# Forgetting attention with a spectral mix: two loads of v on hardware queues, and two late copies exchanged between ScalarE and VectorE

## The chip, the cores and the metric

The kernel runs on one core of one Trainium2 chip. The metric is the device time of one execution in microseconds. A core has five engines that run beside each other, each with its own instruction queue: TensorE (PE; its weight loads are shown as PEld), VectorE (DVE), ScalarE (ACT), GpSimd (POOL) and SyncE (SP), which here only issues transfers. All transfers run on 16 DMA engines. Transfers are issued from GpSimd ([...]the profile calls that queue q0), from SP (q1) or from ScalarE (q10). Matrix products land in PSUM, and VectorE or ScalarE copy them from there to SBUF.

## The reference

```python
scores = scale * np.matmul(q, k.transpose(0, 1, 3, 2))        # B=8, H=8, S=576, head_dim 64
cum = np.cumsum(np.log(np.clip(f, 0.0001, 1.0)), axis=-1)
scores = np.where(causal, -1e9, scores + cum[:, :, :, None] - cum[:, :, None, :])
attn = softmax(scores)
x = np.matmul(attn, v)            # then as (B, S, H * D): 8 x 576 x 512
X = np.fft.rfft(x, axis=1)        # the first 64 modes are kept
Yr = Xr @ w_r - Xi @ w_i          # for each mode m: one 512 x 512 matrix w_r[m] and w_i[m]
Yi = Xr @ w_i + Xi @ w_r
y = np.fft.irfft(Y, n=S, axis=1)
u = x + y
return u + np.maximum(u @ w_ch, 0.0)
```

All inputs and the output are float32. q, k, v are 9.4 MB each, the two mode weights 67 MB each, the output 9.4 MB.

## The kernel before

**Attention.** The 64 pairs of batch and head are worked in 32 steps; two steps (the two heads of a pair of heads) share one load of k, q and v, so there are 16 such loads, called pairs here: pair 0 is loaded first, then pair 1, and so on. `emit_loads(pr)` (L260) issues the three transfers of pair `pr` into a staging buffer; three staging buffers rotate, and the one of pair 1 lies in the tile wx, which later holds weights. k and q are cast to bf16 on the way, which only GpSimd's queue does here; v is kept in float32 and is not cast. Of v, only pair 0 goes another way: line 270 sends it to SP's queue (L271). Everything else goes through `pool_dma` (L91), which also pins the transfer into the written order of GpSimd's queue. The first use of a pair is a copy that rearranges k, q or v (L482, L486), followed by transposes (L500) and their copies out of PSUM (L513, L515, L517), scores (L552), the exponential on ScalarE (L559), a triangular mask on VectorE (L574) and the product with v (L597), which VectorE divides by its sum into `x_all` (L608, L619).

**The head.** Before the first pair is used, the decay is computed from f: f is loaded by SP (L292), ScalarE takes the logarithm (L344), VectorE the running sum (L349), and after transposes and subtractions ScalarE takes two exponentials (L389, L412). The result scales v at L486.

**Modes.** The weights w_r and w_i come as 128 transfers of 512 KB of bf16 (cast from 1 MB of float32; the last two of them in halves) through GpSimd's queue, in an order fixed in `tile_of` and `emit_w_load`, into nine rotating buffers. `emit_modes` (L170, L186) multiplies one such pair of tiles with the transformed x. The first tiles are loaded beside the attention. A weight's buffer comes free when its products are done, and GpSimd waits for that, and for the landing of an earlier transfer, before it issues the next.

**The inverse transform and the last product.** z = x @ w_ch is computed in parallel to the last weights (`emit_xw`, `XW`, L838, L845). The modes' results y, and y @ w_ch, come in parts: the early part is added to `x_all` and `XW` in `emit_part` (L887, L888) while weights still arrive. What remains for the end is the late part of y, in three groups. The last group depends on the last weights. Its rows are made at L1017 by `y_rows`: four transposes into the PSUM tile ply (y itself, bf16) and four products into plw (y @ w_ch, called the z rows here, float32). Each holds 128 partitions: 16 rows for each of the eight batch entries. They must go to the tile `yy`, to partitions that differ with the batch entry. For batch 0 a copy does that directly (`row_slot(0, t, ...)`, t = 0 for y, 1 for z); for the other seven the whole 128 rows are copied to a stage `yls[0]` and moved from there by 14 transfers of 16 KB, issued by GpSimd (`emit_moves`, L801): first the two for batch 1, then the rest. Then 20 jobs produce the output: TensorE adds x and the late part of y into the PSUM tiles pu and pz (L806), ScalarE copies pu (L974), VectorE computes max(pz, 0) + u (L981), and SP and ScalarE store it (L988, L993).

**What sets the order.** Each engine runs its instructions in one fixed order. Except where `tc.keep_in_program_order` pins an instruction behind the one written before it on its engine (GpSimd's transfers, the rearranging copies of the first three pairs, the last modes' products), a planner of the compiler may move an instruction ahead of others that are ready later by its own estimate. It also adds the waits: an instruction that reads a PSUM tile waits for what wrote it, and two engines that touch one PSUM tile are kept apart.

The lines that the change replaces:

```python
                if nm == "v" and pr < 1:
                    nc.sync.dma_start(dst, ap)
...
        nc.vector.tensor_copy(row_slot(0, 0, H2, H4), ply[0:H4, :])
        nc.scalar.copy(yls[0][:, 0, :], ply[:, :])
        emit_moves(yls[0], H2, 1, 0, nc.gpsimd)
        run(terms(jobs[0], ps, 0, "y"))
        nc.vector.tensor_copy(row_slot(0, 1, H2, H4), plw[0:H4, :])
        nc.vector.tensor_copy(yls[0][:, 1, :], plw[:, :])
        emit_moves(yls[0], H2, 1, 1, nc.gpsimd)
```

Of the kernel before, what the change touches and what calls it, by code (L numbers as in the profile page):

```python
# [21 lines left out]
def kernel(  # L22
# [11 lines left out]
    nc = tc.nc  # L34
# [55 lines left out]
    def pool_dma(dst, src):  # L90
        tc.keep_in_program_order(nc.gpsimd.dma_start(dst, src))  # L91
# [133 lines left out]
    with ExitStack() as actx:  # L225
# [34 lines left out]
        def emit_loads(pr):  # L260
            dc, bp, _ = steps[2 * pr]
            for nm, src in (("k", k), ("q", q), ("v", v)):
                one = src[2 * bp, 2 * dc, :, :]
                dst = QKVst[pr % STG][nm][:, :, :, :].rearrange("p b r d -> p b (r d)")
                ap = bass.AP(
                    tensor=one.tensor,
                    offset=one.offset,
                    ap=[[NR * Dh, 128], [H * S * Dh, 2], [1, NR * Dh]],
                )
                if nm == "v" and pr < 1:  # L270
                    nc.sync.dma_start(dst, ap)  # L271
                else:
                    pool_dma(dst, ap)

# [2 lines left out]
        def scratch(parts, *dims):  # L277
# [13 lines left out]
        ft = ftf[:BH, :]  # L291
        nc.sync.dma_start(ft[:], f.rearrange("b h s -> (b h) s"))  # L292
        emit_loads(0)
        nc.gpsimd.memset(trimask[:, :], 1.0)
        nc.gpsimd.affine_select(
# [15 lines left out]
            channel_multiplier=-1,  # L311
        )
        emit_loads(1)
        emit_w_load(0)
        emit_w_load(1)
# [378 lines left out]
        for s in range(NS + 1):  # L694
            pr, h = s // 2, s % 2
            if s == 0:
                emit_loads(STG - 1)
# [35 lines left out]
    with ExitStack() as bctx:  # L733
        bsb = bctx.enter_context(tc.tile_pool(name="bsb", bufs=1))
        YTe = bsb.tile([128, NDC, B, HM], BF16, name="YTe")
        H2, H4 = HM // 2, HM // 4
# [42 lines left out]
        def row_slot(b, t, r0, n):  # L779
            p0 = HM * ((b + t) % 2) + r0  # L780
            return yy[p0 : p0 + n, 1, b // 2, t, :]
# [17 lines left out]
        def emit_moves(yl, r0, b, t, eng):  # L799
            p0 = H4 * b  # L800
            ins = eng.dma_start(row_slot(b, t, r0, H4), yl[p0 : p0 + H4, t, :])  # L801
            if eng is nc.gpsimd:
                tc.keep_in_program_order(ins)
# [147 lines left out]
        def terms(job, ps, t, what):  # L951
            b, _, nb = job
            rows = [[] for _ in range(2 * nb)]
            for tt, i, o, hs, src, basis in pieces(job):
                if tt != t:
                    continue
                p = ps[t][o, i, :]
                rows[2 * i].append((p, ident_bf[hs, hs], src, True))
                rows[2 * i + 1].append((p, basis, yy[hs, 1, b // 2, t, :], False))
            return [r for k, r in enumerate(rows) if "xy"[k % 2] in what]  # L960

        def run(*lists, pin=False):
            for k in range(max(len(l) for l in lists)):
                for l in lists:
                    for a in l[k] if k < len(l) else ():
                        ins = add(*a)
                        if pin:
                            tc.keep_in_program_order(ins)
# [45 lines left out]
        ply = psL.tile([128, D], F32, tag="A", name="ply")  # L1014
        ply = ply[:, 0 : D // 2].bitcast(BF16)
        plw = psL.tile([128, D], F32, tag="A", name="plw")
        y_rows(YTl, 0, ply[:, :], plw[:, :])  # L1017
        nc.vector.tensor_copy(row_slot(0, 0, H2, H4), ply[0:H4, :])
        nc.scalar.copy(yls[0][:, 0, :], ply[:, :])
        emit_moves(yls[0], H2, 1, 0, nc.gpsimd)  # L1020
        run(terms(jobs[0], ps, 0, "y"))
        nc.vector.tensor_copy(row_slot(0, 1, H2, H4), plw[0:H4, :])
        nc.vector.tensor_copy(yls[0][:, 1, :], plw[:, :])
        emit_moves(yls[0], H2, 1, 1, nc.gpsimd)
        for b in range(2, B):
# [60 lines left out]
```

The softmax here doesn't subtract the row's maximum and nothing guards it: scores larger than these inputs give would overflow.

## Time and profile before

| | |
|---|---|
| six runs | median 438.12 us (436.19 to 439.43) |
| the profiled execution | 438.14 us, span 436.4 us |
| mean granted TensorE clock | 0.834 |
| PE busy | 368.2 us (84% of the span) |
| DVE busy | 263.5 us (60%) |
| ACT busy | 225.3 us (52%) |
| POOL busy | 129.1 us (30%) |
| transfers | 97.37 MB at the destination; 163.73 MB read from HBM, 9.44 MB written to it |

The profile is of one execution, and its times count from the start of the span. The slices of the page cut the span into 40 equal parts of 10.9 us; a digit is the busy share in tenths. A line of the timeline gives the start, the duration, the engine (SPq, ACTq and POOLq are the engine's queue, where a transfer's issue counts), the line of the program, the operation with its output and inputs, the number of instructions merged, and in brackets the idle time of the engine just before and what ended it. A line of the table by stretches gives the stretch, its length, the busy time and count of instructions of PE, PEld, DVE, ACT and POOL, the granted clock of TensorE, the share in which the 16 DMA engines were busy, and GB/s at the destination; the share can pass 1, because packets of one engine overlap. A wait for several events is put down to the one that came last.

### The profile page before, as it was taken

To read this page: it belongs to the slowest core of one execution; us is meant where nothing else is said; L and a number is where in the kernel's file an instruction comes from. 1 tells how busy PE (TensorE), PEld (TensorE's weight loads), DVE (VectorE), ACT (ScalarE), POOL (GpSimd) and SP (SyncE) were. 2 spreads that over 40 slices of the span, in tenths; PEclk is the share of its full clock that TensorE was granted. 3 is DMA by queue.
4 is the path that set the end of the run, shared out by engine and by line. 5 is a ranking of instruction groups with operands and counts; after the bars stand their busy time and mean duration, and the time that the engine had idled before them with its cause. 6 is when DMAs were issued, how large, how long until landed. Compare 5 with 4: busy or idle time off the path is not lost.

```text
span 436.4 us, 12232 instructions
## 1 busy us (share of the span) xinstructions
PE 368.2 (84%) x5265; PEld 250.9 (57%) x5265; DVE 263.5 (60%) x658; ACT 225.3 (52%) x340; POOL 129.1 (30%) x202
## 2 busy tenths in 40 slices
PE   2687699999897978878878798799999988798993
PEld 1454566776666656666656676666655544454451
DVE  5687788877555654556656577624323655553874
ACT  3688377875635446364364654143444444542762
POOL 7333332153233232332332222232232232200500
PEclk9997699998856755587566879599999999998997
DMA  8999999999999999999999999999999999993697
GB/s 188 232 236 244 231 237 238 236 214 234 236 211 237 229 219 237 211 236 235 212 237 211 212 211 211 213 210 210 211 213 210 211 211 211 211 210 77 237 390 262
DMA packets 50693, 97.37 MB, mean 223 GB/s; under 512 B 3760, under 2 KB 12944, under 8 KB 50640
## 3 DMA queue, kind: packets, MB, share of 16 engines
q0 software_dynamic: 46688, 86.16, 100.7%
q1 hardware_dynamic: 3632, 9.91, 6.1%
q8 instruction: 41, 0.67, 0.6%
q10 hardware_dynamic: 320, 0.52, 0.5%
q14 instruction: 12, 0.10, 0.1%
HBM read 163.73 MB, written 9.44 MB: 397 GB/s over the span
## 4 chain that ended last, share of the span: by engine, by line
PE 31%; DMA 30%; ACT 12%; DVE 9%; issue 4%; POOL 2%; DVEq 0%; POOLq 0%; ACTq 0%
DMA wb<-in_moe_w_i_dram 25%; ACT E L559 8%; PE pav L597 7%; PE ps L552 6%; PE A L186 5%; PE tp L500 5%; DMA stv<-in_v_dram 3%; PE px L640 2%; PE vp L524 2%; ACT KT L513 2%; DVE QTs L515 2%; ACT VT L517 1%; DVE XT L654 1%; DMA yy<-yl 1%; POOL yy L801 1%
## 5 line engine op out<-in xcount | busy, mean ns | idle before, releaser
L559 ACT ACTIVATE E<-ps 128x1024 bf16<-128x1024 f32 (+1 forms) x128 | 101.5, 854 | 25.9 <-PE ps L552 16.6
L91 POOL DMA_DIRECT2D wb<-in_moe_w_r_dram x64 | 42.5, 665 | 132.7 <-PE A L186 28.6
L186 PE MATMUL A<-XT,wb 128*128 128x16 bf16 x1984 | 70.0, 181 | 11.2 <-DMA wb<-in_moe_w_i_dram 6.6
L186 PEld LDWEIGHTS <-wb 128*128 128x128 bf16 x1984 | 63.4, 99 | 25.4 <-issue 11.4
L552 PE MATMUL ps<-QTs,KT 64*128 64x64 bf16 (+4 forms) x384 | 58.0, 326 | 14.4 <-ACT E L559 13.1
L91 POOL DMA_DIRECT2D wb<-in_moe_w_i_dram x64 | 42.5, 664 | 73.4 <-DMA wb<-in_moe_w_i_dram 32.2
L597 PE MATMUL pav<-va,E 128*128 128x65 bf16 (+1 forms) x1088 | 56.2, 212 | 4.4 <-DVE x_all L619 3.6
L597 PEld LDWEIGHTS <-E 128*128 128x128 bf16 (+1 forms) x1088 | 46.5, 117 | 17.6 <-issue 7.1
L574 DVE TENSOR_TENSOR E<-E,trimask 128x256 bf16<-128x256 bf16 (+2 forms) x128 | 37.2, 302 | 19.5 <-ACT E L559 19.3
L517 ACT COPY VT<-tp 128x640 bf16<-128x640 bf16 (+1 forms) x32 | 23.1, 758 | 32.5 <-PE tp L500 32.4
L845 ACT CAST XW<-pxw 128x512 bf16<-128x512 f32 x36 | 20.7, 587 | 35.9 <-PE pxw L838 35.8
L552 PEld LDWEIGHTS <-KT 64*128 64x128 bf16 x384 | 19.5, 100 | 31.0 <-issue 22.4
L888 ACT CAST XW<-pB 128x512 bf16<-128x512 f32 x36 | 21.0, 586 | 29.6 <-PE pB L806 22.4
L838 PE MATMUL pxw<-wch,yy 128*128 128x512 bf16 x144 | 36.0, 388 | 0.0
L887 DVE CAST x_all<-pA 128x512 bf16<-128x512 f32 x36 | 24.9, 692 | 15.4 <-PE pA L806 14.5
L513 ACT COPY KT<-tp 128x640 bf16<-128x640 bf16 (+1 forms) x32 | 22.2, 757 | 22.1 <-PE tp L500 22.1
L515 DVE COPY QTs<-tp 128x640 bf16<-128x640 bf16 (+1 forms) x32 | 23.2, 766 | 14.2 <-PE tp L500 14.1
L619 DVE TENSOR_TENSOR x_all<-pav,rcp 128x384 bf16<-128x384 f32 x64 | 29.1, 455 | 0.8
L608 DVE RECIPROCAL rcp<-pav 128x6 f32<-128x6 f32 x64 | 12.1, 190 | 24.1 <-PE pav L597 23.3
L151 DVE TENSOR_TENSOR YTe<-A,Yacc 128x128 bf16<-128x128 f32 x16 | 5.9, 367 | 33.4 <-PE A L186 33.4
L981 DVE SCALAR_TENSOR_TENSOR uo<-pz,uo 128x1024 f32<-128x1024 f32 (+1 forms) x21 | 21.9, 1069 | 5.0 <-PE pu L806 1.6
L806 PEld LDWEIGHTS <-ident_bf 64*64 64x64 bf16 (+1 forms) x300 | 15.3, 108 | 15.5 <-issue 7.6
(141 smaller groups left out, 641.4 us busy)
## 6 DMA issues: line engine op xcount, KB each, us to landing
wb<-in_moe_w_r_dram POOLq DMA_DIRECT2D x62, 512.0 KB, 16.6
wb<-in_moe_w_i_dram POOLq DMA_DIRECT2D x62, 512.0 KB, 17.5
out_dram<-uo SPq DMA_DIRECT2D x15, 512.0 KB, 4.2
stv<-in_v_dram POOLq DMA_DIRECT2D x10, 576.0 KB, 15.2
stk<-in_k_dram POOLq DMA_DIRECT2D x11, 288.0 KB, 15.1
stq<-in_q_dram POOLq DMA_DIRECT2D x11, 288.0 KB, 15.1
wx<-in_v_dram POOLq DMA_DIRECT2D x5, 576.0 KB, 15.1
wx<-in_k_dram POOLq DMA_DIRECT2D x5, 288.0 KB, 14.7
```

The source lines that it names most:

```text
L91: tc.keep_in_program_order(nc.gpsimd.dma_start(dst, src))
L186: nc.tensor.matmul(A[:, eb, mi, :], lhsT=w_of(mi, eb * 128), rhs=x_of(m), start=(i == 0), stop=(i == len(terms) - 1),)
L513: nc.scalar.copy(rows(KTs[pr % 2][:, :, 0:S]), tv)
L515: nc.vector.tensor_copy(rows(QT[pr][:, :, :]), tv)
L517: nc.scalar.copy(rows(VTs[pr % 2][:, :, 0:S]), tv)
L552: nc.tensor.matmul(ps[:, b, o : o + n], lhsT=KTs[pr % 2][bs, h, jb * 128 : (jb + 1) * 128], rhs=QT[pr][bs, h, jb * 128 + c0 : jb * 128 + c ...
L559: nc.scalar.activation(E[:, :, piece * 512 : piece * 512 + w], ps[:, :, 0:w], ACT.Exp, scale=scale,)
L574: nc.vector.tensor_tensor(dg, dg, tr, ALU.mult)
L597: nc.tensor.matmul(pav[64 * half : 64 * half + w, slot, :], lhsT=E[:, b, c : c + (w - 1) * st + 1 : st], rhs=va[:, jb, b, :], start=(n == ...
L619: nc.vector.tensor_tensor(xo, pi, ri, ALU.mult)
L838: nc.tensor.matmul(pxw[:, :], lhsT=xT[:, eb, i * 128 : (i + 1) * 128], rhs=wch[:, eb, :], start=(eb == 0), stop=(eb == NDC - 1),)
L887: nc.vector.tensor_copy(xs, pA[:, :])
```

## The change

v of pair 0 goes from SP's queue to ScalarE's (the Activation queue). v of pair 1 goes from GpSimd's queue to SP's, where it follows f; it leaves GpSimd's pinned order. At the end, the copy of the whole y rows from ply to the stage goes from ScalarE to VectorE, and the copy of batch 0's z rows from plw goes from VectorE to ScalarE. Sizes and types of all transfers and copies stay as they were.

```diff
-                if nm == "v" and pr < 1:
-                    nc.sync.dma_start(dst, ap)
+                if nm == "v" and pr < 2:
+                    (nc.sync if pr else nc.scalar).dma_start(dst, ap)
                 else:
                     pool_dma(dst, ap)
...
         nc.vector.tensor_copy(row_slot(0, 0, H2, H4), ply[0:H4, :])
-        nc.scalar.copy(yls[0][:, 0, :], ply[:, :])
+        nc.vector.tensor_copy(yls[0][:, 0, :], ply[:, :])
         emit_moves(yls[0], H2, 1, 0, nc.gpsimd)
         run(terms(jobs[0], ps, 0, "y"))
-        nc.vector.tensor_copy(row_slot(0, 1, H2, H4), plw[0:H4, :])
+        nc.scalar.copy(row_slot(0, 1, H2, H4), plw[0:H4, :])
         nc.vector.tensor_copy(yls[0][:, 1, :], plw[:, :])
         emit_moves(yls[0], H2, 1, 1, nc.gpsimd)
```

## The prediction

> **What bounds the kernel now.** I read the page's DMA slices first, because all weights come in once and nothing else in the page runs near its limit for long.
>
> ```profile
> DMA  8999999999999999999999999999999999993697
> GB/s 188 232 236 244 231 237 238 236 214 234 236 211 237 229 219 237 211 236 235 212 237 211 212 211 211 213 210 210 211 213 210 211 211 211 211 210 77 237 390 262
> ...
> q0 software_dynamic: 46688, 86.16, 100.7%
> ```
>
> From the second slice to the 36th the 16 DMA engines never fall below nine tenths. The queue that GpSimd fills (q0) is alone 100.7% of their span. A table of busy time by stretches says the same more finely:
>
> ```profile
> 0.00:2.00 2.00, 0.00 (x0) 0.00 (x0) 1.05 (x8) 1.20 (x1) 0.87 (x5) 1.00 0.00 0
> ...
> 240.00:280.00 40.00, 32.45 (x556) 25.80 (x554) 27.66 (x74) 19.00 (x32) 10.07 (x15) 0.76 1.12 211
> ...
> 394.00:398.00 4.00, 3.78 (x70) 2.39 (x70) 1.89 (x4) 1.17 (x2) 0.00 (x0) 1.00 0.65 128
> ```
>
> The last two columns are the DMA share and GB/s. With weights alone the rate is a flat 211 GB/s of bf16 written, so a 512 KB load takes 524 KB / 211 = 2.48 us; yet the page gives such loads 16.6 and 17.5 us from issue to landing, so some six others stand ahead of each. The whole input as a sum: 163.73 MB read, less 9.44 MB of v and 0.15 MB of f, is 154.1 MB of fp32 that is cast on the way, 77 MB written at 211 GB/s, 365 us; v at the 385 GB/s shown below 24.5 us; f 0.4 us. Together 390 us, in the 397 us between the first traffic (2.2 us) and the last weight (399.45 us). Most of the rest is the end, where the engines finish unevenly (share 0.65). So **one unbroken stream of loads sets the time up to 399.5 us**, and 37 us of output follow. The chain of waits names PE, ScalarE and VectorE for half the span, but it can follow GpSimd's waits for free buffers, which cost nothing while six loads are queued. Only two places can then matter: how soon the stream fills, and what follows its end.
>
> The start, as the GB/s line of the first 20 us in bins of 0.5 us, and as a timeline:
>
> ```profile
> GB/s 0 0 0 0 92 272 230 290 334 313 200 198 201 203 210 201 205 210 198 219 235 373 424 358 255 210 209 217 209 213 201 213 221 213 201 213 213 221 205 201
> ```
>
> ```profile
> 0.80 0.60 SPq L292 DMA_DIRECT2D Yacc<-in_f_dram  x1
> ...
> 1.33 0.87 POOL L91 DMA_DIRECT2D stk<-in_k_dram  x1 [0.82 <-POOLq L1070]
> ...
> 1.47 0.56 SPq L271 DMA_DIRECT2D stv<-in_v_dram  x1
> ...
> 3.75 0.68 ACT L344 ACTIVATE Yacc<-Yacc 64x576 f32<-64x576 f32 x1 [1.67 <-DMA Yacc<-in_f_dram]
> ...
> 5.30 0.73 POOL L91 DMA_DIRECT2D wx<-in_v_dram  x1
> ```
>
> Until 5.0 us only SP's two transfers flow (f, v of pair 0), at 230 to 334 GB/s; from 5 us GpSimd's cast loads run at their usual 200 to 210. The step 373, 424, 358 near 11 us is v of pair 1 passing through GpSimd's queue: uncast, 385 GB/s in the mean, 590 KB in 1.5 us.
>
> The end:
>
> ```profile
> 400.97 0.41 DVE L1018 COPY yy<-ply 16x512 bf16<-16x512 bf16 x1 [0.85 <-PE ply L787]
> ...
> 401.42 0.59 ACT L1019 COPY yl<-ply 128x512 bf16<-128x512 bf16 x1 [3.97 <-DVE yy L1018]
> ...
> 402.60 0.51 POOL L801 DMA_DIRECT2D yy<-yl  x1 [17.80 <-ACT yl L1019]
> 402.68 0.68 DVE L1022 CAST yy<-plw 16x512 bf16<-16x512 f32 x1 [1.29 <-PE plw L791]
> ...
> 403.39 0.69 DVE L1023 CAST yl<-plw 128x512 bf16<-128x512 f32 x1
> 403.43 0.56 PE L806 MATMUL pu<-x_all,ident_bf 64*64 64x512 bf16 x1
> ...
> 403.68 2.02 ACT L974 COPY uo<-pu 128x512 f32<-128x512 f32 x3 [1.67 <-PE pu L806]
> ...
> 404.38 6.22 POOL L801 DMA_DIRECT2D yy<-yl  x13 [1.26 <-DVE yl L1023]
> ...
> 404.80 3.72 DVE L981 SCALAR_TENSOR_TENSOR uo<-pz,uo 128x512 f32<-128x512 f32 x4 [0.71 <-ACT uo L974]
> ```
>
> TensorE runs almost without a gap from 400.33 us to about 408 us, at a granted clock of 0.57 in 400 to 404 us. The first uo on VectorE waits for the products, and from there VectorE is busy 21.9 of 26.1 us.
>
> [...]where SP's last packets and GpSimd's first ones meet, after 5 us, the rate is no higher than later with GpSimd's queue alone. [...]SP's issue at 0.80 is followed by traffic in the bin from 2.0 us, and GpSimd's k, issued at 1.33, by the cast rate only from 5.0. [...]L1019 only reads ply, as L1018 does, and starts 0.04 us after L1018 ends. Its new counterpart on plw will be serial too.
>
> **The change, part by part.** *v of pair 0 to the Activation queue.* One issue, 0.56 us, leaves SP and goes to ScalarE at 0.80 us. Behind it there stand the table load (1.28 us) and the Ln at 3.75 us: 0.80 + 0.56 + 1.28 = 2.64, so the 1.1 us left hide it; without that cover it would cost 0.56 us of ScalarE. The transfer starts some 0.67 us sooner (1.47 - 0.80).
>
> *v of pair 1 to SP.* GpSimd loses one issue of 0.73 us, free because GpSimd's issues wait for landings. The transfer now flows beside f and v of pair 0 from about 2.9 us. What that is worth is the bandwidth unused before 5 us; the trace does not show two hardware queues at once. In 2.0 to 5.0 us, 1531 GB/s-bins x 0.5 = 766 KB moved. Upper end: 385 GB/s from 2.5 us on, 46 + 2.5 x 385 = 1009 KB, 243 KB more, 0.63 us of stream. Middle: 334, the best that one queue reached, 46 + 835 = 881 KB, 0.30 us. Lower end: no gain, and, as the bytes are the same, no loss. I take **-0.45 us**, which passes whole to the end since the stream is unbroken.
>
> Who is delayed: k and q of pair 0 may now share with 590 KB more, 1.5 us at most. k landed 6.1 us after 1.33, at 7.5, q at 8.9; first read at 11.52 and 11.90 us: hidden. v of pair 1 is first read at 20.34 us. f shares with v of pair 0 from its start: 147 KB / 385 = 0.4 us later if they alternate, 1.5 us if all of v goes ahead. This moves Ln and the whole head of the attention. It reaches the end only if a buffer comes free too late for the stream. The tightest place is GpSimd's 11 us wait before the load issued at 82.18 us: it landed after 7.0 us, of which 2.5 are its transfer and 1.6 what a small load on idle engines takes (the first yl), so 2.9 us of cover. 0.4 later and 0.45 sooner use 0.9 of it; the worst, 1.5 + 0.63 = 2.1, also fits. Cost 0.
>
> *The two copies.* L1019 on VectorE: a 128x512 bf16 read of PSUM took it 0.41 us (L859), against 0.59. It would end near 401.8 instead of 402.01. GpSimd's first yl issue may come 0.2 us sooner, but the second, for which it must wait next, is tied to plw. L1022 on ScalarE has no row; the nearest is 128x512 fp32 to bf16 at 0.59 (L888)[...]. I take 0.59 against 0.68. The z rows come at 403.27 instead of 403.36; TensorE is busy until 403.43 either way: nothing. The following L1023 on VectorE starts 0.1 us sooner, and with it GpSimd's 13 issues at 404.38. ScalarE is free before 403.68. Between 0 and -0.1 us, or +0.1 if the crossing between engines costs more than the 0.04 us above; I take **-0.05**.
>
> Sum: 438.14 (profiled execution; 436.4 span and 1.7 around it) - 0.45 - 0.05 = **437.6 us**. That execution lies 0.02 from the median of 438.12.
>
> **The rivals.** *Nothing reaches the end* (0.22): the second hardware queue brings no rate. Then 438.1. For it: SP's 334 GB/s is already 87% of 385. Against: the 230 bin.
> *Faster* (0.12): the 3.3 us of TensorE from 400.33 to 403.63 ran at 0.57 of its clock; at full clock 3.3 x 0.43 = 1.4 us less. If the shifted end falls outside that dip, with the full 0.63 and 0.1, 436.0. Against: nothing in the change addresses the clock.
> *Slower* (0.09): the order on ScalarE is planned, not written out, at these lines. If its z rows are queued behind the three uo copies (403.68 to 405.70), they end at 406.29 instead of 403.36; pz, the first uo and thirteen yl transfers wait 2.9 us: 438.14 - 0.45 + 2.93 = 440.6. It decides from the third copy ahead of it; behind two it gives 439.8. Against: its operand is ready at 402.64, a microsecond before theirs.
>
> **Numbers.** Forecast 0.57, rivals 0.22, 0.12, 0.09. A measurement of this kernel tells about 0.5% (2.2 us) from no change. Forecast and first rival lie within; half of the others' edges spill: faster 0.12, same 0.78, slower 0.10. The six runs spread by 3.2 us[...]. Range 435.8 to 439.4.
>
> **What would show it.** Right: over 300 GB/s in every bin from 2.5 to 5 us, the last weight landing 0.3 to 0.6 us sooner, L1019 at 0.41 us, the ScalarE row copy ending by 403.3 less the same shift. Wrong: a bin under 200 GB/s between 12 and 390 us, which means that the stream broke and compute binds; the first uo more than 5.4 us after the last weight; or a different order of instructions around 82 us.

## The result, and the profile after

The changed kernel takes 441.49 us (median of 15 runs) against 437.35 us for the kernel before (34 runs on the same chip). The ratio, 1.010 with a 95% interval of 1.0077 to 1.0124, leaves out two of the 15 runs (446.92 and 447.61 us), which were slow ones. By the ratio the changed kernel is 4.4 us slower. The forecast was 437.6 us, with 439.4 as its upper edge. The profiled execution took 441.11 us, with a span of 439.4 us.

The page's slices, DMA share and GB/s at the destination, of the changed kernel:

```profile
DMA  8999999999999999999999999999999999994697
GB/s 200 211 236 240 234 236 238 197 188 236 211 237 236 211 238 229 219 236 221 227 236 212 211 211 212 212 211 211 211 212 211 211 211 211 211 211 95 225 378 281
...
q0 software_dynamic: 46544, 85.57, 99.9%
```

The eighth and ninth slices (77 to 99 us) read 197 and 188 where before read 236 and 214. That is a hole in the middle, and in tenths of share it doesn't show at all.

The start, GB/s in bins of 0.5 us over the first 20 us, and the lines of the timeline that answer to those shown of before:

```profile
GB/s 0 0 0 32 240 295 350 392 226 173 293 288 265 221 170 210 221 205 198 207 196 212 205 203 217 210 215 209 213 213 205 217 213 209 209 209 209 217 217 197
```

```profile
0.81 0.43 ACTq L271 DMA_DIRECT2D stv<-in_v_dram  x1
0.81 0.60 SPq L292 DMA_DIRECT2D Yacc<-in_f_dram  x1
...
1.47 0.56 SPq L271 DMA_DIRECT2D wx<-in_v_dram  x1
...
5.69 0.68 ACT L344 ACTIVATE Yacc<-Yacc 64x576 f32<-64x576 f32 x1 [3.14 <-DMA Yacc<-in_f_dram]
```

The stream starts sooner and reaches 392 GB/s, but falls to 173 GB/s at 4.5 us. The logarithm (ACT L344, called Ln below) waits for f until 5.69 us, 1.94 us longer than before (3.75).

The hole itself, GB/s in bins of 0.75 us from 70 to 100 us, first of before, then of after:

```profile
GB/s 208 210 210 213 210 213 221 202 210 208 209 213 194 215 252 355 337 264 242 191 209 217 210 216 210 208 210 213 224 205 205 210 209 207 205 205 245 289 322 340
```

```profile
GB/s 230 197 213 210 216 205 213 210 213 208 217 202 218 196 221 298 367 297 244 210 139 98 12 0 117 164 218 197 210 210 205 188 150 180 218 199 197 208 201 203
```

Before never falls under 191. After has 12 and 0 GB/s near 87 us, and what is lost there doesn't come back. What opened the hole stands in GpSimd's and TensorE's timelines, first of before, then of the changed kernel:

```profile
80.86 1.02 PE L186 MATMUL A<-XT,wb 128*128 128x16 bf16 x32
...
82.18 0.62 POOL L91 DMA_DIRECT2D wb<-in_moe_w_r_dram  x1 [11.04 <-PE vp L524]
```

```profile
85.28 1.17 PE L186 MATMUL A<-XT,wb 128*128 128x16 bf16 x32
...
86.76 0.62 POOL L91 DMA_DIRECT2D wb<-in_moe_w_r_dram  x1 [15.11 <-PE vp L524]
...
91.32 0.62 POOL L91 DMA_DIRECT2D wb<-in_moe_w_r_dram  x1 [3.33 <-PE ps L552]
```

This is the load that the prediction called the tightest place. It was issued at 82.18 us before; now GpSimd waits 15.11 us for its buffer and issues it 4.58 us later. The transfers that were queued had run out by then. The load belongs to the tenth pair of weights, and there are nine buffers. It follows the end of the first 32 products of the modes (A, L186) by 0.30 us in all 17 traces of this document; these products free the buffer of the first pair, and they in turn need the transformed x of the attention. (By the profile vp, L524, came last, right behind them.) The last weight lands at 403.20 us instead of 399.45, 3.75 us later.

The end, from the timeline of after:

```profile
405.52 0.41 DVE L1018 COPY yy<-ply 16x512 bf16<-16x512 bf16 x1 [0.65 <-PE ply L787]
405.97 0.42 DVE L1019 COPY yl<-ply 128x512 bf16<-128x512 bf16 x1
...
406.38 0.57 ACT L1022 CAST yy<-plw 16x512 bf16<-16x512 f32 x1 [3.60 <-PE plw L791]
...
406.99 0.69 DVE L1023 CAST yl<-plw 128x512 bf16<-128x512 f32 x1 [0.60 <-ACT yy L1022]
...
407.09 0.51 POOL L801 DMA_DIRECT2D yy<-yl  x1 [18.95 <-ACT yy L1022]
```

The exchanged copies take 0.42 and 0.57 us. From the last weight to the end it is 36.2 us against 36.95 before, so the whole loss lies ahead of the last weight. The 0.8 us gained behind it can't be credited to the copies: TensorE was granted its full clock in 402 to 406 us, against 0.78 before, and over the traces below this stretch lasts from 34.4 to 37.3 us.

### The profile page after: what moved, and what is told of

Read it like the earlier page. It is cut to its first block, busy times and chain, and to the rows that moved or that the text cites. A ratio compares the mean times of both kernels' runs of the same rounds, so it can differ in the third digit from the quotient of the medians.

```text
span 439.4 us, 12235 instructions
## 1 busy us (share of the span) xinstructions
PE 365.5 (83%) x5265; PEld 248.4 (57%) x5265; DVE 262.8 (60%) x658; ACT 225.4 (51%) x340; POOL 129.3 (29%) x201
## 4 chain that ended last, share of the span: by engine, by line
PE 36%; DMA 26%; ACT 12%; DVE 9%; issue 4%; DVEq 0%; POOL 0%; ACTq 0%
DMA wb<-in_moe_w_i_dram 26%; ACT E L559 8%; PE pav L597 7%; PE ps L552 7%; PE A L186 6%; PE tp L500 5%; PE pz L806 3%; PE px L640 2%; PE vp L524 2%; ACT KT L513 2%; DVE QTs L515 2%; PE pu L806 2%; DVE uo L981 2%; DVE XT L654 1%; ACT VT L517 1%
## 5 line engine op out<-in xcount | busy, mean ns | idle before, releaser
L186 PE MATMUL A<-XT,wb 128*128 128x16 bf16 x1984 | 70.0, 181 | 13.6 <-DMA wb<-in_moe_w_i_dram 9.0
L186 PEld LDWEIGHTS <-wb 128*128 128x128 bf16 x1984 | 63.5, 100 | 27.8 <-issue 11.8
L552 PE MATMUL ps<-QTs,KT 64*128 64x64 bf16 (+4 forms) x384 | 60.7, 328 | 19.3 <-ACT E L559 18.0
L574 DVE TENSOR_TENSOR E<-E,trimask 128x256 bf16<-128x256 bf16 (+2 forms) x128 | 37.3, 302 | 21.6 <-ACT E L559 21.0
L888 ACT CAST XW<-pB 128x512 bf16<-128x512 f32 x36 | 20.9, 586 | 34.3 <-PE pB L806 28.6
L806 PEld LDWEIGHTS <-ident_bf 64*64 64x64 bf16 (+1 forms) x300 | 16.2, 110 | 15.7 <-issue 8.8
```

The source lines that it names most:

```text
L186: nc.tensor.matmul(A[:, eb, mi, :], lhsT=w_of(mi, eb * 128), rhs=x_of(m), start=(i == 0), stop=(i == len(terms) - 1),)
L552: nc.tensor.matmul(ps[:, b, o : o + n], lhsT=KTs[pr % 2][bs, h, jb * 128 : (jb + 1) * 128], rhs=QT[pr][bs, h, jb * 128 + c0 : jb * 128 + c ...
L574: nc.vector.tensor_tensor(dg, dg, tr, ALU.mult)
L806: return nc.tensor.matmul(p, lhsT=lhsT, rhs=rhs, start=first, stop=not first, skip_group_check=True)
```

## The experiments

Two explanations of the late load were set against each other. The first, **late f**: v of pair 0 on the second queue delays f, and with f the head of the attention. The second, **the planned order**: in the traces TensorE's order of instructions is unchanged by the copies or by v of pair 0 alone, but changed from about 26 us on as soon as v of pair 1 leaves GpSimd's list. The table gathers all runs; "Ln" is its start, "load" the issue of the weight load that before has at 82.18, "clock" the mean granted TensorE clock in 36 to 60 us of the profiled execution. Each ratio is to runs of before on the same chip. The three columns of shifts give, for one transfer, the mean over the 16 DMA engines of when its part landed, less the same in before: for the first weight (about 15 us), for the load just ahead of the one in question, and for the third after it.

| kernel | Ln, us | load, us | clock | first weight | ahead | after it | ratio to before (95%) |
|---|---|---|---|---|---|---|---|
| before | 3.75 | 82.18 | 0.72 | 0 | 0 | 0 | 1 |
| after | 5.69 | 86.76 | 0.57 | +0.47 | +0.38 | +3.64 | 1.0100 (1.0077 to 1.0124) |
| e1_v0_act | 5.95 | 83.37 | 0.72 | -0.02 | -0.09 | +0.84 | 1.0024 (1.0007 to 1.0042) |
| e2_f_late | 6.25 | 85.45 | 0.79 | +0.35 | +0.33 | +2.44 | 1.0035 (1.0008 to 1.0062) |
| e3_v1_sp | 3.62 | 85.93 | 0.58 | +0.23 | +0.21 | +2.64 | 1.0050 (1.0032 to 1.0069) |
| e4_f_act | 5.71 | 89.42 | 0.54 | -0.10 | -0.20 | +6.43 | 1.0088 (1.0057 to 1.0120) |
| e5_v1_sp_order | 3.46 | 82.51 | 0.72 | +0.32 | +0.33 | +0.40 | 1.0024 (1.0010 to 1.0038) |
| e6_after_order | 6.01 | 83.49 | 0.72 | +0.24 | +0.27 | +0.93 | 1.0061 (1.0039 to 1.0083) |
| e7_late_copies | 3.65 | 82.80 | 0.79 | +0.11 | +0.12 | +0.64 | 0.9999 (0.9982 to 1.0016) |
| e8_loads_only | 6.01 | 88.41 | 0.62 | +0.24 | +0.18 | +5.29 | 1.0105 (1.0067 to 1.0143) |
| e9_v0_after_f | 4.19 | 83.10 | 0.72 | -0.10 | -0.09 | +0.71 | 1.0001 (0.9982 to 1.0021) |
| e10_all_after_f | 3.87 | 84.08 | 0.79 | -0.07 | -0.11 | +1.60 | 1.0008 (0.9989 to 1.0027) |
| e11_order_only | 3.58 | 83.59 | 0.67 | +0.10 | +0.02 | +0.86 | 1.0030 (1.0014 to 1.0046) |
| e12_order_more | 3.78 | 78.08 | 1.00 | +0.11 | +0.08 | +0.15 | 0.9996 (0.9987 to 1.0005) |
| e13b_v0_act_cover | 5.63 | 82.08 | 1.00 | +0.45 | +0.43 | +0.44 | 1.0005 (0.9987 to 1.0022) |
| e14b_f_late_cover | 6.96 | 82.48 | 1.00 | +0.66 | +0.67 | +0.68 | 1.0008 (0.9995 to 1.0022) |
| e15b_all_iotas_first | 5.64 | 79.59 | 1.00 | +0.09 | +0.12 | +0.22 | 0.9990 (0.9973 to 1.0007) |

The load, the clock and the shifts are of one execution each, the ratios of many. e7 (+0.64 us, but 0.9999) and e10 (+1.60, but 1.0008) show how far one execution may lie from its ratio; that of e10 is the longest of its 14 runs.

**The parts alone.** e1 moves only v of pair 0; e2 puts f behind it on SP; both keep the order of before. e3 moves only v of pair 1, to SP, which brings the order of after; e4 does the same with f on the Activation queue.

```diff
 e1:  -   nc.sync.dma_start(dst, ap)            # pr < 1
      +   nc.scalar.dma_start(dst, ap)
 e2:  -   nc.sync.dma_start(ft[:], f...);  emit_loads(0)
      +   emit_loads(0);  nc.sync.dma_start(ft[:], f...)
 e3:  -   if nm == "v" and pr < 1:
      +   if nm == "v" and pr < 2:
 e4:  as e3, and
      -   nc.sync.dma_start(ft[:], f...)
      +   nc.scalar.dma_start(ft[:], f...)
```

> The kernel before with one edit: v of pair 0 on ScalarE's queue; v of pair 1 stays in GpSimd's queue and the late copies stay. The planned order of TensorE, VectorE and GpSimd is that of before. Theory A (late f alone): f lands behind v, the logarithm starts near 5.7 us instead of 3.75, the stream of loads breaks near 87 us and the run is about 3 us slower (440.5). Theory B (planned order alone): f may be late, but the order is the old one, so the load issued at 82.2 us comes only about 2 us later, the stream does not break, and the time is that of before (within 1 us). Theory C (both are needed, as the cover of about 2.5 us must be used up): the same as B here, a shift of 1.9 us at 82 us with no break.

> The kernel before with f and v of pair 0 exchanged on SP's queue: v first, then f. One hardware queue only, all planned orders as before. Theory A (late f alone): the logarithm about 1.9 us later, stream broken near 87 us, about 440.5. Theories B and C: the logarithm equally late, the load of 82.2 us issued some 2 us later, no break, time as before within 1 us.

> Both v on SP's queue behind f, nothing on ScalarE's queue, old late copies. The planned order of TensorE and GpSimd is that of the changed kernel. f is first and should land as before, so the logarithm starts at 3.75 us. Theory A (late f alone): as before, within 1 us. Theory B (planned order alone): the issue of 82.2 us comes at least 4 us later, the stream breaks, about 440.5. Theory C (both): the shift at 82 us is what is left of 4.6 without 1.9, about 2.6 us, right at the cover: a break of 0 to 0.6 us and a time 0 to 1 us above before.

> f alone on ScalarE's queue, both v on SP's queue; planned order of TensorE and GpSimd that of the changed kernel. ScalarE's queue delivered first in the changed kernel, so f should come at 3.5 us or sooner. Theory A (late f alone): as before, within 1 us. Theory B (order alone): about 440.5. Theory C (both): 0 to 1 us above before, with a shift of about 2.4 us at 82 us. If the two hardware queues are served one after the other, v of pair 0 starts only when f is done.

Neither explains it alone: a late f in the old order costs 0.24 and 0.35%, the new order with f in time costs 0.50%. e4 brought a surprise. f was issued on the Activation queue at the same moment as v of pair 0 on SP, and f was again the later one, Ln at 5.71 us. So here it isn't the queue that decides. In after, e1 and e4 both issues start at the same moment, but v's takes 0.43 to 0.44 us and ends near 1.25 us, while f's takes 0.55 to 0.60 and ends at 1.35 to 1.41. In these traces the one whose issue ended first went through first. A split of the traffic by queue from 1.5 to 4.4 us in after:

```profile
q10 hardware_dynamic: 272, 0.59, 63.4%
q1 hardware_dynamic: 80, 0.16, 19.3%
```

The Activation queue (q10) has moved all of v by 4.2 us, in 272 packets as the profile counts them; SP's first traffic (q1) comes at 3.6 us, when the packets of 84% of v have begun. What lets so much of v go ahead of f is not shown by these runs.

**The order, held fixed.** In e5 and e6 GpSimd repeats one tiny iota (an instruction that writes a row of counted numbers) 17 times, behind the first weight loads. With that the planner gives TensorE, VectorE and ScalarE the order of before, instruction for instruction (in e6 but for the exchanged copies). The repeats took 3.4 us of GpSimd in e5 and 4.3 in e6 and delayed no landing: in e5 the shift is +0.32 us for the first weight, issued ahead of them, and +0.33 for the load before the one in question. e7 has only the copies, e8 only the two loads.

```diff
 e5: e3, and
 e6: the whole change, and
 +   for _ in range(17): tc.keep_in_program_order(nc.gpsimd.iota(s_i[:, 0:4], ...))
     tc.keep_in_program_order(nc.gpsimd.iota(s_i[:, 0:4], ...))
```

> Before with v of pair 1 on SP behind f and v of pair 0, as in e3, but with 17 tiny repeated iotas on GpSimd (about 0.1 us each, their result is overwritten by itself) in the place of the issue that left it. With them the planner gives TensorE, VectorE and ScalarE the order of before, instruction for instruction. If the reordering is what cost e3 its 0.5%: back to before, 437.0 to 437.6 us, ratio 0.999 to 1.001, and the load near 82 us is issued within 1 us of before (82.2). If what costs is the queue move itself (v of pair 1 sharing the engines with k and q of pair 0): the same as e3, 439.6, ratio 1.005, load near 86.

> The whole change (both v on hardware queues, f late, both late copies exchanged) with the same 17 tiny iotas, so that the order of TensorE, VectorE and ScalarE is that of before but for the exchanged copies. If the order and the late f add up: only the late f is left, the ratio of e1, 1.002 (438.3 us), load near 82 us issued 1 to 3.3 us late. If the late f alone explained the loss: unchanged, 1.010 (441.5). If order and late f only hurt together: 1.000.

> Before with only the two late copies exchanged; the rest of the order is that of before. All theories of the start: 437.4 us, ratio 0.999 to 1.001; the prediction's step gives -0.05 us. The rival that the copies cost something at the end (GpSimd's first issue from the stage waits for ScalarE): 438.0 or more, ratio 1.0015 and up.

> The change without the exchanged copies: v of pair 0 on the Activation queue, v of pair 1 on SP. If the copies are neutral: as the whole change, ratio 1.009 to 1.010 (441.4 us). If they cost: 0.5 us less than that, ratio 1.008 or below.

The change of order accounts for 1.0100 less 1.0061, 0.39% or 1.7 us of the 4.4, and for 0.26% in e3 against e5. (What is left, 0.61%, goes when f is no longer late: e10 below.) With the intervals of both ratios these are 0.1 to 0.7% and 0.0 to 0.5%, so the sign is shown and the size is rough. The copies cost nothing that can be measured, as e7 shows directly, and e8 loses as much as the whole change. Where the new order falls behind is seen on ScalarE. From the timeline of e3:

```profile
33.79 2.85 ACT L559 ACTIVATE E<-ps 128x1024 bf16<-128x1024 f32 x3 [0.95 <-PE pav L597]
36.66 1.28 ACT L450 ACT_TABLE_LOAD   x1
...
38.95 1.28 ACT L559 ACT_TABLE_LOAD   x1
40.24 1.19 ACT L559 ACTIVATE E<-ps 128x128 bf16<-128x128 f32 x2
42.51 1.02 ACT L559 ACTIVATE E<-ps 128x1024 bf16<-128x1024 f32 x1 [1.07 <-PE ps L552]
...
46.04 0.28 ACT L559 ACTIVATE E<-ps 128x128 bf16<-128x128 f32 x1
```

And of before:

```profile
31.94 3.25 ACT L559 ACTIVATE E<-ps 128x128 bf16<-128x128 f32 x5
35.21 1.28 ACT L450 ACT_TABLE_LOAD   x1
...
37.52 1.28 ACT L559 ACT_TABLE_LOAD   x1
38.81 1.94 ACT L559 ACTIVATE E<-ps 128x1024 bf16<-128x1024 f32 x2
...
42.19 1.19 ACT L559 ACTIVATE E<-ps 128x1024 bf16<-128x1024 f32 x2
```

The sines of the basis, with a table load on either side, begin 1.45 us later, and the exponentials of this group end at 46.3 instead of 43.4 us. The first transformed block of x (L676) ends at 48.2 us in e3 against 44.1 in before and 44.3 in e5. Against e5, which has the same transfers as e3 in the old order (table load at 35.52 us), the sines are still 1.1 us late, and the clock was still 0.99 in 30 to 36 us of e3: so much is the order itself. Then a second difference comes in, the clock. The table by stretches, 36 to 60 us, of before, after, and e15b, a kernel described below:

```profile
36.00:60.00 24.00, 18.40 (x201) 12.92 (x202) 17.52 (x53) 14.33 (x23) 8.36 (x13) 0.72 1.13 235
```

```profile
36.00:60.00 24.00, 18.46 (x165) 11.45 (x164) 15.06 (x42) 13.32 (x20) 8.20 (x12) 0.57 1.13 235
```

```profile
36.00:60.00 24.00, 20.20 (x288) 13.68 (x286) 20.63 (x61) 20.17 (x31) 8.17 (x13) 1.00 1.13 235
```

In the clock column of the table above the 17 traces fall into groups by their order: 0.54 to 0.62 in the order of after, 0.72 to 0.79 in that of before (on three chips), 0.67 in e11, and 1.00 in the four with all iotas first. In the same stretch TensorE is busy for 17.5 to 20.9 of 24 us, so a lower clock can hold up the attention and with it the load. An order may thus cost or gain by what it puts first, by the clock that was granted with it, or by both. No run changed one without the other, so beyond these 1.1 us that stays open.

**Is f late because of the queue?** In e9 and e10 v of pair 0 stays on the Activation queue, behind a logarithm of a tiny tile; e10 has the rest of the change too, in the order of before (with the 17 iotas of e6).

```diff
 +   nc.scalar.activation(held, held0, ACT.Ln)     # both pinned
     nc.scalar.dma_start(dst, ap)                  # v of pair 0
```

> Before with v of pair 0 on the Activation queue, as in e1, but held there until f is surely ahead: ScalarE first takes the logarithm of a tiny dummy tile (the table load comes with it), then issues v at about 2.3 us. TensorE and VectorE keep the order of before. If the two hardware queues serve what was handed over first, whole: f lands as in before, Ln at 3.6 to 3.9 us, ratio 0.999 to 1.001. If a queue of ScalarE beside one of SP delays f or the stream as such: Ln later than 5 us and the ratio of e1, 1.002.

> e6 (the whole change in the order of before) with v of pair 0 held behind f in the same way; v of pair 1 stays on SP. If late f and the share of v of pair 1 are separate costs: the ratio of e5, 1.0024, and Ln before 4 us. If two hardware queues together cost something of their own: the ratio of e6, 1.006.

The hold did less than meant, and by that showed more. From the timeline of e9:

```profile
0.81 0.59 SPq L292 DMA_DIRECT2D Yacc<-in_f_dram  x1
...
0.98 0.46 ACTq L271 DMA_DIRECT2D stv<-in_v_dram  x1
...
2.10 0.21 ACT L271 ACTIVATE held<-held 128x8 f32<-128x8 f32 x1
...
4.19 0.68 ACT L345 ACTIVATE Yacc<-Yacc 64x576 f32<-64x576 f32 x1 [1.89 <-DMA Yacc<-in_f_dram]
```

v was issued at 0.98 us, not 2.3: here the queue's issue didn't wait for the logarithm. It begins 0.17 us after f's and ends some 0.05 us after it, and f is ahead again, Ln at 4.19 (3.87 in e10). The ratios go back to 1.0001 and 1.0008.

**The order alone, and the cover.** "Cover" is how much later the load may be issued before the queued transfers run out. e11 and e12 leave every transfer where before has it and only write GpSimd's three iotas sooner.

```diff
 e11: emit_loads(1); emit_w_load(0); <iotas>; emit_w_load(1)
 e12: emit_loads(1); <iotas>; emit_w_load(0); emit_w_load(1)
 before: emit_loads(1); emit_w_load(0); emit_w_load(1); <iotas>
```

> Before with its queues unchanged; only GpSimd's three iotas are written ahead of the second weight pair instead of behind it. No transfer changes its queue, but the planner gives a different order from about 24 us on (VectorE's basis work is taken up earlier). If a reordering of that stretch costs by itself: the load near 82 us is issued over 1 us later and the ratio is 1.002 to 1.005. If only the queues matter: 1.000.

> As e11, with the iotas ahead of both first weight pairs: again only the planned order differs, by more of TensorE's instructions than in e11. Same two cases: ratio 1.002 to 1.005 with a later load near 82 us if the order costs, 1.000 if only the queues matter. If either of e11 and e12 is faster than before, the order of before is not the best one and the sign of a reordering is a matter of luck.

e11 costs 0.30% with no change to any queue. With e12's order, and the full clock that came with it, the load goes out at 78.08 us, 4.1 us sooner. Yet the time is that of before, 0.9996. Sooner was worth nothing here and later costs, which is what a stream that is just fed looks like. So the last three kernels put the late f, in both ways, and the whole change into such an order.

```diff
 e13b: e1  + iotas first, as in e12
 e14b: e2  + iotas first
 e15b: the whole change + iotas first
```

> e1 (v of pair 0 on the Activation queue, f late by 2.2 us) in the order of e12, instruction for instruction, where the load near 82 us has about 4 us more cover. If f late costs only through that load: 436.8 to 437.2 us, ratio 0.999 to 1.001, no bin under 190 GB/s near 86 us. If it costs on its own: the ratio of e1, 1.0024.

> e2 (f behind v of pair 0 on SP, late by 2.5 us) in the order of e12. If the cover decides: 0.999 to 1.001; the stream starts 0.35 us later in e2, so up to 1.001 is left. If the late f costs on its own: the ratio of e2, 1.0035.

> The whole change, with all its queues and copies, and GpSimd's three iotas written ahead of the first weight pairs, as in e12. The order is near that of e12, not equal (1294 of some 10500 instructions of TensorE differ in place). If the cover decides and this order gives it (load near 82 us issued before 82.5): ratio 0.999 to 1.002, against 1.010 for the change as it stands. If the load is late again by over 3 us: 1.005 or more. If the queues cost on their own: 1.005 to 1.006, with the load early.

e15b from 70 to 100 us, in the same bins as above:

```profile
GB/s 223 210 227 197 208 218 210 205 208 210 209 208 206 204 278 345 284 289 219 218 208 213 210 216 216 221 194 213 208 218 210 208 205 213 218 199 212 306 329 301
```

```profile
79.59 0.62 POOL L91 DMA_DIRECT2D wb<-in_moe_w_r_dram  x1 [7.71 <-PE ps L552]
```

The whole change, with f as late as in after (Ln at 5.64 us), loses nothing that can be measured: ratio 0.9990. There is no hole, because the load is out at 79.59 us. Its runs had a mean clock of 0.861 against 0.840 for before, but the eight of them at 0.841 to 0.856 also took 436.7 us in the median. The late f costs nothing measurable either way (1.0005, 1.0008): it makes the load 4.0 and 4.4 us later than in e12, and so within 0.3 us of before. So the late f and the order have no price of their own that shows here; they cost by making this load late. For the 0.24% of e5 that is not shown: its load went out at 82.51 us, and its trace lost 0.3 us ahead of that load and hardly anything at it. No version was faster than before by more than its interval.

## Why the prediction was wrong, point by point

**The bound** was right: the stream of loads sets the time. e12 agrees, where a load 4.1 us sooner gained nothing (0.9996), and so does after, where a hole in the stream was not made up (the last weight landed 3.75 us later). The prediction also named the hole as its first sign of error, and the hole came.

**"It reaches the end only if a buffer comes free too late ... Cost 0"** is the step that failed. The place was right, the tightest load; both terms of the sum at that place were mis-sized.

What uses the cover up was taken as 0.9 us, 2.1 at worst. The load went out 4.58 us late, and the stream ahead of it was 0.38 us late, so 4.2 us were used. The prediction carried f's own delay to the load one for one and put nothing in for the order or the clock. With f alone late (Ln by 2.20 and 2.50 us) the load was 1.19 us late in e1 and 3.27 in e2; with the new order and f in time (e3) it was 3.75 us late.

The cover was taken as 2.9 us, with 1.6 us for the latency of a small load. When the stream has run dry (after, e2, e3, e4, e8), the load in question is complete on its first engine 4.35 to 4.56 us after its issue and on the last after 4.97 to 5.12. Before had 5.20 and 7.04. As an estimate from these, the engine that is done first has 0.8 us of cover, the last one 2.0. With 2.9 us a hole of 1.3 us would have been left; with 0.8 to 2.0 it is 2.2 to 3.4, and the stream lost 3.26 us (+0.38 to +3.64). Loads only 0.6 and 1.2 us late (e7, e1) lost 0.5 and 0.9 us. Most of that, 0.5 and 0.6 us, was lost not at this load but at the next pair, which goes out 4.6 us behind it and whose cover wasn't worked out.

**"f: 0.4 us later if they alternate, 1.5 if all of v goes ahead"**, of which 0.4 was taken: measured 1.94 us in Ln, outside even the upper end. Nearly all of v went ahead (84% had begun before f's first bytes), and the rate in its bins climbs from 240 to 392 GB/s rather than being 385 at once. In the old order this is worth 0.24% (e1).

**"-0.45 us ... as the bytes are the same, no loss"**: the sign is not there. With v of pair 1 on SP the first weight landed between 0.10 us sooner (e4) and 0.47 later (after), never more than 0.1 sooner. Kernels that leave v of pair 1 alone spread as widely, from 0.10 sooner (e9) to 0.66 later (e14b), so this is no gain rather than a shown loss. In after, what the early start moves by 4 us is lost in the bins of 226 and 173 GB/s, where v of pair 0 is through and the next transfers only begin, and v of pair 1 passes in bins of 293 to 170 where 385 was hoped for. That a second queue brings no rate, the prediction had itself read in the trace of before: in 5 to 7 us, where SP's last packets run beside GpSimd's, the bins hold 200, 198, 201 and 203 GB/s, with GpSimd's alone behind them 198 to 219. These runs agree with it (after reaches 392 GB/s with both hardware queues at work, GpSimd's queue alone reached 424 before), and the -0.45 did not heed it. At a fixed order the move costs 0.24% in e5; e10, which has it too, is at 0.08% with an interval that holds 0. Whether the move has a price of its own is not settled.

**"GpSimd loses one issue of 0.73 us, free"** holds for GpSimd's own time (its first weight load goes out at 5.30 us instead of 6.03), but the move had a second effect: with one issue fewer on GpSimd's list the planner gave TensorE, VectorE and ScalarE another order. The prediction named a different order as a sign of error but gave it no price. It is 1.7 us of the 4.4 (0.3 to 3.1), with the clock that came with it.

**The copies** were right: 0.42 and 0.57 us against 0.41 and 0.59 taken, and a sum that can't be measured (0.9999). So were the issue on ScalarE, which took 0.43 us and was hidden behind the wait for f (3.14 us idle before Ln), and the first rival's argument that the second queue brings no rate. Its 438.1, like the other rivals, missed that the start can also be lost. The slower rival, with 440.6 the nearest number, had its place at the end; z's row copy ran ahead of the three uo copies (406.38 us, the first of them 406.98), and nothing of it came, so that its number is near by chance.

## What to carry to other kernels

Where a stream is only just fed, size the cover at the place with the longest wait, on the engine that runs dry first, with a latency measured on the same queue; being sooner there gained nothing here, being later cost nearly all of it. Follow a delay of the head to that place along every engine, since here it did not arrive one for one. Moving an issue from one queue to another can change who goes first and, where a planner sets the order, the order of much that comes after it, so compare the two programs' orders before pricing the move, and compare the granted clock stretch by stretch before calling an order quick. A loss found in one part (here a late f) is best tested where the cover is ample: if it vanishes there, look for what supplies the cover.

## What the hardware showed that was not expected

Two hardware queues that were given transfers at the same moment shared very little: in after the packets of 84% of the 590 KB of v had begun before the first bytes of f, and f was late whichever of the two queues v was on (Ln at 5.69 us in after, 5.95 in e1, 5.71 in e4, against 3.75 before). An issue of v that began 0.17 us and ended 0.05 us after f's turned it round (e9); which of the two moments decides isn't shown. The time from the issue of a 512 KB cast load to its landing on the first DMA engine was 4.35 to 4.56 us where the stream had run dry, against the 1.6 us in all of a small uncast one that the prediction had used. And TensorE's mean granted clock in 36 to 60 us went from 0.54 to 1.00 with the order of nearly the same instructions, where the mean over the whole profiled execution hides it: 0.834 before, 0.84 after.
